# Turning the last 64 queries and keys in a shared bank, scoring in two steps, and a new order within a block of attention

## The chip, the cores and the metric

The kernel runs on one core of one Trainium2 chip. The metric is the device time of one execution in microseconds (us). Every comparison is between runs of the kernel before and after the change on the same chip. The core has five engines that matter here, each with its own instruction stream that it works off in order: TensorE (PE, with its weight loads shown apart as PEld), VectorE (DVE), ScalarE (ACT), GpSimd (POOL) and SyncE (SP), which here only issues DMAs. They wait for each other through semaphores.

## The reference, cut to what matters

```python
# batch 8, heads 8, sequence 576, head dimension 64, all float32
scores = scale * np.matmul(q, k.transpose(0, 1, 3, 2))          # scale 1/8
thresh = np.max(scores, axis=-1, keepdims=True) - tau
scores = np.where(scores >= thresh, scores, -1000000000.0)
scores = scores - np.max(scores, axis=-1, keepdims=True)
attn = np.exp(scores)
attn = attn / (np.sum(attn, axis=-1, keepdims=True) + 1e-09)
attn_out = np.matmul(attn, v)
x = attn_out.transpose(0, 2, 1, 3).reshape(4608, 512)
h = np.maximum(x @ w_in, 0.0)                                     # 512 -> 2048
out = h * h @ w_out                                               # 2048 -> 512
```

## The kernel before, in words

There are three stages, one after the other: attention, the hidden layer (x @ w_in, relu, square) and the output layer. The change touches only attention.

**Pairs, slots and blocks.** Two heads are worked at a time: 32 pairs. The 576 queries of a pair are cut into four tiles of 128 and a last one of 64 (`BLK`, `NB = 5`), so attention is 160 slots, numbered `n = 5 * pair + t`. Five slots of one pair are called a block here, and `s` stands for `n mod 5`. `slot(n)` (L531) is a software pipeline written out by hand: in slot n the scores of slot n+3 are computed, the softmax of n+2 is begun, that of n+1 ended, the weights of n-1 are transposed and the product with v of n-2 is made. The order of the calls in `slot` is the order of the instructions on every engine.

**What a slot issues.** The names that the text uses are these:

- *w*, *W* and *R*: `turn_part(n - 1, ...)`. W transposes the first head's four tiles of weights into a PSUM bank and copies them out on ACT (L427, L429, L432), w does the same for the second head, and R transposes the last 64 columns of both heads (L405). For the last tile of a pair (t = 4), w does nothing.
- *values*: `values_and_load(n - 2)` multiplies with v (L457, L462) into part 0 of a bank named `pvR`; R puts its transpose in part 1 of that bank, and one ACT copy (L408, or L411 with L413 or L417) takes both parts out. In the slots with s = 1 it also issues the loads of a later v (L290, L292).
- *q turn*, *k turn*, *rest turn*: the generator `turn` for the next pair transposes its 512 first queries (bank `pqk`, L303, copied and scaled on ACT by L308), its 512 first keys (L303, L306) and then the last 64 of both together (bank `pqkr`, L311, copied by L312 and L313). GpSimd then copies the 64 keys of the two heads to the diagonal blocks of `kdiag` (L316). q and k turn are in slot s = 0, the rest turn late in slot s = 1, and after it `load` asks SP for the queries and keys of the pair after next (L278, L279).
- *main* and *diagonal*: `ahead(n + 3)` calls `scores`, which makes two main products (L341), one per head, against 512 keys, and one product against `kdiag` for the last 64 keys of both heads (L345). Head 0 ends up in columns 0 to 575 and head 1 in columns 960 to 1535 of a tile `sc` of three banks. For t = 4 there is no diagonal product but four small main ones.
- `stage` and `second` step the softmax generators: two maxima on DVE (L357), a threshold on POOL (L362), two exponentials on ACT (L369), two masked sums on DVE (L374), a tiny add on POOL (L378), a reciprocal on DVE (L380) and two scalings on POOL (L389).
- `convert1` to `convert6` turn one of 32 chunks of the FFN weights from float64 to float32 (a new chunk every second slot; in slots 0 to 34 and 76 to 110). `fetch` loads the raw chunk (L181), `convert1` is its first reader, on ACT (L201). `sums_step` is one POOL addition of weight blocks per slot (L130 or L133) in slots 35 to 79 and 111 to 155.

**Buffers.** [...] two `sc` tiles of three banks, and two single banks (`b_pool`) that every transpose and every product with v takes in turn. A new use of such a bank waits until ACT has copied out the use before the last. So the order in which the banks are asked for, together with ACT's order, decides who waits for whom.

Of the kernel before, what the change touches and what calls it, by code (L numbers as in the profile page):

```python
# [10 lines left out]
FP32 = mybir.dt.float32  # L11
# [37 lines left out]
def kernel(  # L49
# [25 lines left out]
    nc = tc.nc  # L75
# [219 lines left out]
    def turn(i):  # L295

        qn, kn, rn = loaded.pop(i)
        qT = sb.tile([P, S], FP32, tag="qT", bufs=2, name="qT")
        kT = sb.tile([P, S], FP32, tag="kT", bufs=2, name="kT")
        for nat, to in ((qn, qT), (kn, kT)):  # L300
            pt = bank([P, FULL, P], "pqk")
            for t in range(FULL):
                nc.tensor.transpose(pt[:, t, :], nat[:, t, :], ident[:, :])  # L303
            flat, to = pt[:, :, :].rearrange("p t m -> p (t m)"), to[:, 0:MAIN]
            if nat is kn:
                nc.scalar.copy(to, flat)  # L306
            else:
                nc.scalar.activation(out=to, in_=flat, func=AF.Identity, scale=qscale[:, :])  # L308
            yield
        pt = bank([P, P], "pqkr")  # L310
        nc.tensor.transpose(pt[:, :], rn[:, :], ident[:, :])  # L311
        nc.scalar.activation(out=qT[:, MAIN:S], in_=pt[:, 0:REST], func=AF.Identity, scale=qscale[:, :])  # L312
        nc.scalar.copy(kT[:, MAIN:S], pt[:, REST:P])  # L313
        for j in range(2):
            rows = ds(j * D, D)
            nc.gpsimd.tensor_copy(out=kdiag[i % 2][rows, ds(j * REST, REST)], in_=kT[rows, MAIN:S])  # L316
        turned[i] = (qT, kT)

    def scores(i, t):

        qT, kT = turned[i]
        m = BLK[t]
        sc = sc_pool.tile([P, 3 * BANK], FP32, tag="sc", name="sc")
        b_main = 2 * BANK


        one_rest = t < FULL  # L330
        for part in range(1 if one_rest else 2):
            for j in range(2):
                rows = ds(j * D, D)
                k0, n = ((0, MAIN), (MAIN, REST))[part]
                if t == FULL:
                    to = sc[rows, ds(k0, n)]
                elif j == 0:
                    to = sc[:, ds(k0, n)]
                else:
                    to = sc[:, ds((b_main, b_main - REST)[part], n)]  # L340
                nc.tensor.matmul(to, qT[rows, ds(t * P, m)], kT[rows, ds(k0, n)], start=True, stop=True)  # L341
        if one_rest:
            to = sc[:, MAIN:S]
            to = bass.AP(tensor=to.tensor, offset=to.offset, ap=[to.ap[0], [b_main - S, 2], [1, REST]])
            nc.tensor.matmul(to, qT[:, ts(t, P)], kdiag[i % 2][:, :], start=True, stop=True)  # L345
        return sc

    def softmax(i, t, sc):

        nj = 2 if t < FULL else 1  # L350
        at = (0, 2 * BANK - REST)[0:nj]
        sm = sb.tile([P, 2], FP32, tag="sm", bufs=3, name="sm")
        nmx = sb.tile([P, 2], FP32, tag="nmx", bufs=3, name="nmx")
        thr = sb.tile([P, 2], FP32, tag="thr", bufs=3, name="thr")
        w = sb.tile([P, 2 * S], FP32, tag="w", bufs=4, name="w")
        for j in range(nj):
            nc.vector.tensor_reduce(  # L357
                out=nmx[:, j : j + 1], in_=sc[:, ds(at[j], S)], axis=AXIS.X, op=ALU.max, negate=True
            )
            if j == nj - 1:  # L360

                nc.gpsimd.tensor_scalar(  # L362
                    out=thr[:, 0:nj], in0=nmx[:, 0:nj], scalar1=-1.0, scalar2=tau_p[:, :], op0=ALU.mult, op1=ALU.subtract
                )
            yield
        for j in range(nj):
            if j:
                yield
            nc.scalar.activation(  # L369
                out=w[:, ts(j, S)], in_=sc[:, ds(at[j], S)], func=AF.Exp, bias=nmx[:, j : j + 1], scale=1.0  # L370
            )
        for j in range(nj):
            yield
            nc.vector.scalar_tensor_tensor(  # L374
                out=w[:, ts(j, S)], in0=sc[:, ds(at[j], S)], scalar=thr[:, j : j + 1], in1=w[:, ts(j, S)],
                op0=ALU.is_ge, op1=ALU.mult, accum_out=sm[:, j : j + 1],
            )
        nc.gpsimd.tensor_scalar(out=sm[:, 0:nj], in0=sm[:, 0:nj], scalar1=1e-9, scalar2=None, op0=ALU.add)  # L378
        yield
        nc.vector.reciprocal(out=sm[:, 0:nj], in_=sm[:, 0:nj])  # L380
        if t == FULL:

            normalize(w[:, S : S + REST], w[:, MAIN:S], sm[:, 0:1])
        for j in range(nj):
            normalize(w[:, ts(j, S)], w[:, ts(j, S)], sm[:, j : j + 1])
        weights[i, t] = w
# [4 lines left out]
    def transposes(n):  # L391
# [9 lines left out]
        def rest():  # L401


            pt, n_ = pending.pop() if pending else (bank([P, 2, P], "pvR"), 0)
            nc.tensor.transpose(pt[:, 1, :], w[:, ds(MAIN, P)], ident[:, :])  # L405
            xr = sb.tile([P, 2, P], FP32, tag="xr", bufs=3, name="xr")
            if t < FULL and n_ == P:
                nc.scalar.copy(xr[:, :, :], pt[:, :, :])  # L408
            else:
                if n_:  # L410
                    nc.scalar.copy(xr[:, 0, 0:n_], pt[:, 0, 0:n_])  # L411
# [4 lines left out]
                        rows = ds(j * REST, REST)  # L416
                        nc.scalar.copy(xr[rows, 1, at], pt[rows, 1, ds(j * REST, REST)])  # L417
            if n_:
                give_x(n - 1, xr)
            rests[i, t] = xr[:, 1, :]  # L420

        def main(j):
            if j and t == FULL:
# [9 lines left out]

        rows_of[n] = {"R": rest, "W": lambda: main(0), "w": lambda: main(1)}

    rows_of, pending, rests = {}, [], {}

    def turn_part(n, part):

# [6 lines left out]
    def values(i, t):  # L446
# [4 lines left out]
        pt = bank([P, 2, P], "pvR")  # L451
        pv = pt[:, 0, 0:n]

        for c in range(FULL):
# [5 lines left out]
        for j in range(2):  # L460
# [4 lines left out]
        pending.append((pt, n))  # L465

    def give_x(n, xr):
        i, t = slots[n]
# [4 lines left out]
    turning = {}  # L473

    def turn_step(i):
        if i in turning:
            if next(turning[i], 0) == 0 and i + 1 < len(pairs):
                load(i + 1)

    def turn_begin(n):  # L480

        i = n // NB + 1
        if n >= 0 and n % NB == 0 and i < len(pairs):
            turning[i] = turn(i)
            next(turning[i])

    def turn_on(n, at):
        if n >= 0 and n % NB == at:
            turn_step(n // NB + 1)

    def values_and_load(n):

# [17 lines left out]
        if n in jobs and slots[n][1] < FULL:  # L510
            next(jobs[n], None)

    def ahead(n):
        if n < len(slots):
            i, t = slots[n]
            jobs[n] = softmax(i, t, scores(i, t))


    PACE = (2, 1)
# [8 lines left out]
        while summing and next(summing[0], 0) == 0:  # L528
            summing.popleft()

    def slot(n):  # L531

        begun = lambda d: starts.get(n - d)
# [4 lines left out]
        while later:  # L538
            to, from_ = later.popleft()
            nc.sync.dma_start(out=to, in_=from_)  # L540
        turn_begin(n)
        convert4(begun(3))
        turn_part(n - 1, "w")
        values_and_load(n - 2)
        convert1(begun(1))
        turn_part(n - 1, "R")
        stage(n + 2)
        stage(n + 1)
        convert3(begun(2))
        turn_on(n, 0)  # L550
        second(n + 1)
        turn_part(n - 1, "W")
        second(n + 2)
        stage(n + 2)
        sums_step()
        convert5(begun(3))
        convert6(begun(4))
        second(n + 2)
        stage(n + 1)
        turn_on(n, 1)  # L560
        ahead(n + 3)
        convert2(begun(1))
        fetch(begun(-1))


    def inner(product, copy, temp, bank, final, tick):
# [274 lines left out]
                    later.append((to[:, :, b, :], o[row][:, :, i, :]))  # L841


    def flush():
        while later:
            to, from_ = later.popleft()
            nc.sync.dma_start(out=to, in_=from_)

    def spread(work, at):

        n = len(work)
# [3 lines left out]
    with tc.manual_schedule():  # L855
        with ExitStack() as stack:
# [8 lines left out]
            turning[0] = turn(0)  # L865
            for _ in range(3):
                turn_step(0)
            load_v(1)
            for n in range(-3, len(slots)):
                slot(n)  # L870
# [3 lines left out]
                if n > 25:  # L874
                    next(xsums, None)
            n = len(slots)
            values_and_load(n - 2)
            for part in "RWw":
                turn_part(n - 1, part)
            values_and_load(n - 1)  # L880
            pt, m = pending.pop()
            xr = sb.tile([P, 2, P], FP32, tag="xr", bufs=3)
            nc.scalar.copy(xr[:, 0, 0:m], pt[:, 0, 0:m])
            give_x(n - 1, xr)
            for _ in range(60):
                sums_step()
            flush()
        banks = ctx.enter_context(tc.tile_pool(name="banks", bufs=1, space=PSUM))

        def reload(at):  # L890
# [32 lines left out]
        for n in range(NSTEP):  # L923
# [17 lines left out]
            def also(m, at):  # L941
# [8 lines left out]
                if at > 4:  # L950
                    squares_due(0)
                if at == 2:
                    flush()
# [5 lines left out]

            work = [None]  # L960
            output_layer(n, also)
        flush()


def as_float(bits):
# [33 lines left out]
```

## Time and profile before

| | |
|---|---|
| median of 3 runs | 1501.11 us (1499.86 to 1501.19) |
| the profiled execution's own time | 1499.22 us |
| its span, first to last instruction | 1497.4 us |
| granted TensorE clock, mean | 0.998 |
| busy in the span: PE, PEld | 1431.0, 1209.3 us |
| busy in the span: POOL, DVE, ACT | 1051.1, 1004.2, 895.8 us |
| attention, to the first product of the hidden layer | 0 to 694.2 us |
| hidden layer, to the first product of the output layer | 694.2 to 1092.8 us |
| output layer | 1092.8 to 1497.4 us |

The start of L405 marks the slots, because R is issued once in each. From one L405 to the next, a block in the middle of attention looks like this:

| from R of slot s to R of the next | 1 to 2 | 2 to 3 | 3 to 4 | 4 to 0 | 0 to 1 | block |
|---|---|---|---|---|---|---|
| us (block from 300.90) | 4.92 | 3.86 | 3.86 | 3.87 | 4.24 | 20.75 |

A profile line of the timeline has the start in us, the duration, the engine, the line of the kernel, the operation with what it writes and reads, how many instructions were merged in the row, and in square brackets how long the engine had been idle before it and what ended that wait. The ends of PE rows are modelled, so distances between PE rows are taken from start to start.

### The profile page before, as it was taken

What the parts mean: (1) busy time and instruction counts of PE and PEld (TensorE: products, weight loads), DVE (VectorE), ACT (ScalarE), POOL (GpSimd) and SP (SyncE); (2) the same over time, 40 slices, a digit from 0 to 9 for tenths busy, and PEclk for the clock granted to TensorE, in tenths of its full rate; (3) what the DMA queues carried; (4) which work ended last, traced back from release to release, by engine and by line L of the source; (5) the groups of instructions that cost most, each with busy time, mean ns of one, the idle gap of its engine ahead of it and who ended that gap; (6) DMA issues with size and microseconds to landing.
All of it is one profiled execution on the core that took longest, in us unless ns stands there. A gap on an engine that the chain in (4) does not pass through costs nothing.

```text
span 1497.4 us, 35275 instructions
## 1 busy us (share of the span) xinstructions
PE 1431.0 (96%) x12880; PEld 1209.3 (81%) x12880; DVE 1004.2 (67%) x2149; ACT 895.8 (60%) x1792; POOL 1051.1 (70%) x1319
## 2 busy tenths in 40 slices
PE   6999899999999999999999999999999999999998
PEld 4656566666655666667999999999999999999998
DVE  5777666667777666665778777788756666555663
ACT  5887777777877777775666566676553333223330
POOL 3777987777776777773675555666587787777775
PEclk9999999999999999999999999999999999999999
DMA  4435223557343222211323334332994432344411
GB/s 109 117 109 149 63 59 91 163 163 227 97 119 103 63 58 51 58 47 49 132 90 117 114 135 141 114 115 105 352 364 142 142 98 82 108 138 142 142 29 29
DMA packets 212955, 176.89 MB, mean 118 GB/s; under 512 B 99888, under 2 KB 161328, under 8 KB 212784
## 3 DMA queue, kind: packets, MB, share of 16 engines
q1 hardware_dynamic: 212784, 174.65, 37.3%
q8 instruction: 102, 1.67, 0.5%
q14 instruction: 69, 0.57, 0.1%
HBM read 105.12 MB, written 69.47 MB: 117 GB/s over the span
## 4 chain that ended last, share of the span: by engine, by line
PE 76%; DVE 8%; ACT 6%; POOL 4%; issue 2%; DMA 2%; SPq 1%; POOLq 0%; ACTq 0%; DVEq 0%
PE po L810 26%; PE ph L687 23%; PE sc L341 8%; PE pvR L457 7%; PE pwT L427 5%; DVE arena L374 4%; PE sc L345 3%; DVE arena L357 3%; ACT arena L369 2%; PE pvR L405 2%; PE pvR L462 1%; POOL arena L389 1%; DVE arena L133 1%; DMA arena<-in_moe_w_in_dram 1%; PE pqk L303 1%
## 5 line engine op out<-in xcount | busy, mean ns | idle before, releaser
L133 POOL TENSOR_TENSOR arena<-arena 128x512 f32<-128x512 f32 (+1 forms) x315 | 377.9, 1222 | 257.0 <-DVE arena L133 220.6
L687 PE MATMUL ph<-arena,w 128*128 128x128 f32 x3528 | 396.6, 275 | 2.4 <-DVE arena L133 1.6
L810 PE MATMUL po<-w,arena 128*128 128x128 f32 x3528 | 396.3, 275 | 2.1 <-ACT arena L601 1.8
L687 PEld LDWEIGHTS ph<-arena,w 128*128 128x128 f32 x3528 | 394.7, 192 | 4.3 <-DVE arena L133 3.9
L810 PEld LDWEIGHTS po<-w,arena 128*128 128x128 f32 x3528 | 394.7, 192 | 3.6 <-ACT arena L601 2.0
L133 DVE TENSOR_TENSOR arena<-ph,arena 128x512 f32<-128x512 f32 x378 | 255.8, 688 | 93.9 <-PE ph L687 63.3
L357 DVE TENSOR_REDUCE arena<-sc 128x1 f32<-128x576 f32 x288 | 217.3, 755 | 145.8 <-PE sc L345 133.6
L374 DVE SCALAR_TENSOR_TENSOR arena<-sc,arena 128x576 f32<-128x576 f32 x288 | 224.3, 812 | 15.1 <-ACT arena L369 13.9
L389 POOL TENSOR_SCALAR arena<-arena 128x576 f32<-128x576 f32 (+1 forms) x320 | 222.8, 705 | 8.4 <-PE sc L341 1.9
L133 DVE TENSOR_TENSOR arena<-po,arena 128x128 f32<-128x128 f32 x378 | 108.1, 290 | 170.2 <-PE po L810 167.0
L369 ACT ACTIVATE arena<-sc,arena 128x576 f32<-128x576 f32 x288 | 200.5, 745 | 24.6 <-DVE arena L357 12.5
L633 ACT COPY c<-arena 128x512 f32<-128x512 f32 (+1 forms) x303 | 172.7, 579 | 61.4 <-DVE arena L130 55.5
L341 PE MATMUL sc<-arena 64*128 64x512 f32 (+2 forms) x768 | 185.1, 573 | 10.9 <-DVE arena L374 8.7
L427 PE MATMUL pwT<-ident,arena 128*128 128x128 f32 x1152 | 177.3, 276 | 15.8 <-ACT arena L417 7.2
L457 PE MATMUL pvR<-arena 128*64 128x128 f32 (+1 forms) x2560 | 163.2, 268 | 21.8 <-ACT arena L313 20.4
L130 POOL TENSOR_TENSOR arena<-arena 128x512 f32<-128x512 f32 (+1 forms) x138 | 174.6, 1265 | 10.0
L130 DVE TENSOR_TENSOR arena<-arena,c 128x512 f32<-128x512 f32 (+1 forms) x267 | 174.7, 662 | 7.4 <-ACT c L633 6.7
L429 ACT COPY arena<-pwT 128x512 f32<-128x512 f32 x256 | 151.2, 591 | 37.2 <-PE pwT L427 25.5
L457 PEld LDWEIGHTS pvR<-arena 128*64 128x64 f32 x2560 | 127.8, 136 | 51.0 <-ACT arena L313 27.8
L427 PEld LDWEIGHTS pwT<-ident,arena 128*128 128x128 f32 x1152 | 131.3, 141 | 28.7 <-ACT arena L417 14.3
L666 ACT ACTIVATE arena<-arena 128x512 f32<-128x512 f32 x144 | 89.9, 624 | 77.6 <-POOL arena L133 77.6
L601 ACT COPY arena<-po 128x128 f32<-128x128 f32 x63 | 16.7, 265 | 180.1 <-PE po L810 178.1
(49 smaller groups left out, 1147.8 us busy)
## 6 DMA issues: line engine op xcount, KB each, us to landing
g<-arena SPq DMA_DIRECT2D x144, 256.0 KB, 2.0
arena<-g SPq DMA_DIRECT2D x144, 256.0 KB, 4.5
w<-w SPq DMA_DIRECT2D x98, 256.0 KB, 4.5
out_dram<-arena SPq DMA_DIRECT2D x72, 128.0 KB, 2.2
arena<-in_q_dram SPq DMA_DIRECT2D x64, 128.0 KB, 2.6
arena<-in_k_dram SPq DMA_DIRECT2D x64, 128.0 KB, 2.9
arena<-in_v_dram SPq DMA_DIRECT2D x32, 256.0 KB, 2.8
arena<-in_moe_w_out_dram SPq DMA_DIRECT2D x16, 512.0 KB, 4.2
```

Source lines behind the costliest of these rows:

```text
L130: e.tensor_tensor(out=out, in0=x, in1=y, op=ALU.subtract)
L133: e.tensor_tensor(out=out, in0=x, in1=y, op=ALU.add)
L341: nc.tensor.matmul(to, qT[rows, ds(t * P, m)], kT[rows, ds(k0, n)], start=True, stop=True)
L357: nc.vector.tensor_reduce(out=nmx[:, j : j + 1], in_=sc[:, ds(at[j], S)], axis=AXIS.X, op=ALU.max, negate=True)
L369: nc.scalar.activation(out=w[:, ts(j, S)], in_=sc[:, ds(at[j], S)], func=AF.Exp, bias=nmx[:, j : j + 1], scale=1.0)
L374: nc.vector.scalar_tensor_tensor(out=w[:, ts(j, S)], in0=sc[:, ds(at[j], S)], scalar=thr[:, j : j + 1], in1=w[:, ts(j, S)], op0=ALU.is_ge, ...
L389: nc.gpsimd.tensor_scalar(out=out, in0=w, scalar1=r, scalar2=1.0, op0=ALU.mult, op1=ALU.mult)
L427: nc.tensor.transpose(pt[:, c, :], w[:, ds(j * (S + REST) + c * P, P)], ident[:, :])
L457: nc.tensor.matmul(pv[rows, :], va[:, j, c, :], wT[:, j, c, 0:n], start=(c == 0), stop=False, skip_group_check=True)
L633: nc.scalar.copy(c, y)
L687: nc.tensor.matmul(to[:, j, :], W_IN[m, k][:, ts(j, P)], of[k][:, m - 1, :], start=(not more and j == 0), stop=True, skip_group_check=True,)
L810: nc.tensor.matmul(to, g[:, j, :], w[:, j, :], start=(not more and j == 0), stop=(j == 3), skip_group_check=True)
```

## The change

The last 64 queries and keys are no longer transposed into a bank of their own. In slot s = 1 they go to a third part of the `pvR` bank, right after R's transpose, and their copies (ACT, then POOL) follow R's copy. The loads of the pair after next are asked for from there. The scores are made in two calls, the diagonal product first and the main products later. The key turn moves to the end of slot s = 0, between the two. Calls within `slot` are put in another order, the tile `w` has three buffers for four, and the finished values wait in a queue with their slot number.

```diff
         kT = sb.tile([P, S], FP32, tag="kT", bufs=2, name="kT")
+        turning[i] = (qT, kT, rn)
...
-        pt = bank([P, P], "pqkr")
-        nc.tensor.transpose(pt[:, :], rn[:, :], ident[:, :])
...
+    def turn_last(i, pt):
+        qT, kT, rn = turning.pop(i)
+        nc.tensor.transpose(pt, rn[:, :], ident[:, :])
+        def then():
+            nc.scalar.activation(out=qT[:, MAIN:S], in_=pt[:, 0:REST], func=AF.Identity, scale=qscale[:, :])
+            nc.scalar.copy(kT[:, MAIN:S], pt[:, REST:P])
+            for j in range(2):
+                rows = ds(j * D, D)
+                nc.gpsimd.tensor_copy(out=kdiag[i % 2][rows, ds(j * REST, REST)], in_=kT[rows, MAIN:S])
+            turned[i] = (qT, kT)
+            if i + 1 < len(pairs):
+                load(i + 1)
+        return then
+
+    def scores_rest(i, t):
+        sc = sc_pool.tile([P, 3 * BANK], FP32, tag="sc", name="sc")
+        if t < FULL:
+            qT, _ = turned[i]
+            to = sc[:, MAIN:S]
+            to = bass.AP(tensor=to.tensor, offset=to.offset, ap=[to.ap[0], [2 * BANK - S, 2], [1, REST]])
+            nc.tensor.matmul(to, qT[:, ts(t, P)], kdiag[i % 2][:, :], start=True, stop=True)
+        return sc
+
+    def scores(i, t, sc):
...
+        for k0, n in ((0, MAIN),) if t < FULL else ((0, MAIN), (MAIN, REST)):
             for j in range(2):
...
+                to = sc[rows, ds(k0, n)] if t == FULL else sc[:, ds(j * 2 * BANK, n)]
                 nc.tensor.matmul(to, qT[rows, ds(t * P, m)], kT[rows, ds(k0, n)], start=True, stop=True)
...
-        w = sb.tile([P, 2 * S], FP32, tag="w", bufs=4, name="w")
+        w = sb.tile([P, 2 * S], FP32, tag="w", bufs=3, name="w")
...
-            pt, n_ = pending.pop() if pending else (bank([P, 2, P], "pvR"), 0)
+            pt, n_, of = pending.popleft() if pending else (bank([P, 3, P], "pvR"), 0, None)
             nc.tensor.transpose(pt[:, 1, :], w[:, ds(MAIN, P)], ident[:, :])
+            then = turn_last(i + 1, pt[:, 2, :]) if t == 0 and i + 1 in turning else None
...
             rests[i, t] = xr[:, 1, :]
+            if then:
+                then()
...
+    TURN_AT = (0, 0)
...
     def slot(n):
...
+        sums_start(n)
+        ask()
         turn_part(n - 1, "w")
+        convert4(begun(n - 3))
+        convert3(begun(n - 2))
+        stage(n + 2)
+        turn_step(n, 0)
         values_and_load(n - 2)
-        convert1(begun(1))
+        convert1(begun(n - 1))
+        stage(n + 1)
+        second(n + 1)
         turn_part(n - 1, "R")
+        second(n + 2)
+        sums_step()
+        turn_part(n - 1, "W")
+        convert6(begun(n - 4))
         stage(n + 2)
+        second(n + 2)
+        fetch(begun(n + 1))
+        convert5(begun(n - 3))
+        ahead(n + 3, 0)
         stage(n + 1)
...
+        turn_step(n, 1)
+        ahead(n + 3, 1)
+        convert2(begun(n - 1))
```

The removed lines of `slot` are those of L538 to L563 above. `ask` is the former `flush`: it issues the DMAs that wait in `later`. `turn_step(n, 0)` is the q turn and `turn_step(n, 1)` the k turn, both in slots with s = 0. The start and the end of attention make the same calls through the new functions.

More of the change, by code (lines that the diff above doesn't have):

```diff
@@ L309, in turn @@
             yield
-        pt = bank([P, P], "pqkr")
[L311 to L319, printed above, removed]
+    def turn_last(i, pt):
[11 more added lines that the diff above has]
+        return then
@@ L324, in scores @@
+    def scores_rest(i, t):
[7 more added lines that the diff above has]
+    def scores(i, t, sc):
         qT, kT = turned[i]
         m = BLK[t]
-        sc = sc_pool.tile([P, 3 * BANK], FP32, tag="sc", name="sc")
@@ L327, in scores @@
-        b_main = 2 * BANK
-        one_rest = t < FULL
-        for part in range(1 if one_rest else 2):
+        for k0, n in ((0, MAIN),) if t < FULL else ((0, MAIN), (MAIN, REST)):
             for j in range(2):
                 rows = ds(j * D, D)
[L334 to L346, printed above, removed]
+                to = sc[rows, ds(k0, n)] if t == FULL else sc[:, ds(j * 2 * BANK, n)]
+                nc.tensor.matmul(to, qT[rows, ds(t * P, m)], kT[rows, ds(k0, n)], start=True, stop=True)
     def softmax(i, t, sc):
@@ L401, in rest @@
         def rest():
-            pt, n_ = pending.pop() if pending else (bank([P, 2, P], "pvR"), 0)
+            pt, n_, of = pending.popleft() if pending else (bank([P, 3, P], "pvR"), 0, None)
             nc.tensor.transpose(pt[:, 1, :], w[:, ds(MAIN, P)], ident[:, :])
+            then = turn_last(i + 1, pt[:, 2, :]) if t == 0 and i + 1 in turning else None
             xr = sb.tile([P, 2, P], FP32, tag="xr", bufs=3, name="xr")
             if t < FULL and n_ == P:
-                nc.scalar.copy(xr[:, :, :], pt[:, :, :])
+                nc.scalar.copy(xr[:, :, :], pt[:, 0:2, :])
             else:
@@ L418, in rest @@
             if n_:
-                give_x(n - 1, xr)
+                give_x(of, xr)
             rests[i, t] = xr[:, 1, :]
+            if then:
+                then()
         def main(j):
@@ L434, in transposes @@
         rows_of[n] = {"R": rest, "W": lambda: main(0), "w": lambda: main(1)}
-    rows_of, pending, rests = {}, [], {}
+    rows_of, pending, rests = {}, deque(), {}
     def turn_part(n, part):
@@ L450, in values @@
         n = BLK[t]
-        pt = bank([P, 2, P], "pvR")
+        pt = bank([P, 3, P], "pvR")
         pv = pt[:, 0, 0:n]
@@ L464, in values @@
             )
-        pending.append((pt, n))
+        pending.append((pt, n, NB * i + t))
     def give_x(n, xr):
@@ L472, with turn_step @@
     slots = [(i, t) for i in range(len(pairs)) for t in range(NB)]
[L473 to L489, printed above, removed]
+    turning, turns = {}, {}
+    TURN_AT = (0, 0)
+    def turn_step(n, at):
+        i, left = divmod(n - TURN_AT[at], NB)
+        i += 1
+        if left == 0 and 0 < i < len(pairs):
+            if at == 0:
+                turns[i] = turn(i)
+            next(turns[i])
     def values_and_load(n):
@@ L511, in second, with ahead @@
             next(jobs[n], None)
[L513 to L516, printed above, removed]
+    def ahead(n, part):
+        if not 0 <= n < len(slots):
+            return
+        i, t = slots[n]
+        if part == 0:
+            jobs[n] = scores_rest(i, t)
+        else:
+            scores(i, t, jobs[n])
+            jobs[n] = softmax(i, t, jobs[n])
     PACE = (2, 1)
@@ L529, in sums_step, with ask, sums_start @@
             summing.popleft()
-    def slot(n):
-        begun = lambda d: starts.get(n - d)
+    def ask():
+        while later:
+            to, from_ = later.popleft()
+            nc.sync.dma_start(out=to, in_=from_)
+    def sums_start(n):
         if n == OUT_SUMS:
@@ L537, in slot, with begun @@
             summing.append(sums(W_IN, SUMS_A, AT_A, lambda m: None))
[L538 to L542, printed above, removed]
+    def begun(n):
+        return starts.get(n)
+    def slot(n):
+        sums_start(n)
+        ask()
         turn_part(n - 1, "w")
+        convert4(begun(n - 3))
+        convert3(begun(n - 2))
+        stage(n + 2)
+        turn_step(n, 0)
         values_and_load(n - 2)
-        convert1(begun(1))
+        convert1(begun(n - 1))
+        stage(n + 1)
+        second(n + 1)
         turn_part(n - 1, "R")
+        second(n + 2)
+        sums_step()
+        turn_part(n - 1, "W")
+        convert6(begun(n - 4))
         stage(n + 2)
+        second(n + 2)
+        fetch(begun(n + 1))
+        convert5(begun(n - 3))
+        ahead(n + 3, 0)
         stage(n + 1)
[L549 to L563, printed above, removed]
+        turn_step(n, 1)
+        ahead(n + 3, 1)
+        convert2(begun(n - 1))
     def inner(product, copy, temp, bank, final, tick):
@@ L841, in output_layer @@
                     later.append((to[:, :, b, :], o[row][:, :, i, :]))
[L844 to L847, printed above, removed]
     def spread(work, at):
@@ L864 @@
             load_v(0)
-            turning[0] = turn(0)
-            for _ in range(3):
-                turn_step(0)
+            for _ in turn(0):
+                pass
+            turn_last(0, bank([P, P], "pqkr")[:, :])()
             load_v(1)
@@ L876, with drain @@
             n = len(slots)
+            def drain():
+                while pending:
+                    pt, m, of = pending.popleft()
+                    xr = sb.tile([P, 2, P], FP32, tag="xr", bufs=3)
+                    nc.scalar.copy(xr[:, 0, 0:m], pt[:, 0, 0:m])
+                    give_x(of, xr)
+            drain()
             values_and_load(n - 2)
@@ L880 @@
             values_and_load(n - 1)
[L881 to L884, printed above, removed]
+            drain()
             for _ in range(60):
                 sums_step()
-            flush()
+            ask()
         banks = ctx.enter_context(tc.tile_pool(name="banks", bufs=1, space=PSUM))
@@ L952, in also @@
                 if at == 2:
-                    flush()
+                    ask()
                 if at == 6:
@@ L961 @@
             output_layer(n, also)
-        flush()
+        ask()
 def as_float(bits):
```

## The prediction

> **What bounds the kernel now.** I read the totals by stage first, then the starts of L405 as a clock for the slots, then the timeline of one block. Totals by stage (length; busy time and instructions of PE, PEld, DVE, ACT, POOL; clock; DMA):
>
> ```profile
> 0.00:694.00 694.00, 638.27 (x5824) 419.93 (x5824) 474.94 (x1090) 506.73 (x1057) 513.22 (x878) 1.00 0.36 100
> 694.00:1088.00 394.00, 392.75 (x3498) 391.23 (x3499) 301.64 (x474) 251.20 (x450) 231.68 (x185) 1.00 0.40 140
> ```
>
> The hidden layer leaves PE no gap. In attention PE is busy 638 of 694 us, so 56 us at most are to be had there, unless PE itself gets less to do, and the change removes no product. No other engine passes 74%. So the question is where PE waits.
>
> An ordinary slot takes 3.86 us from R to R, and its pieces, start to start, fill it: W 0.53, main 1.06, diagonal 0.33, w 0.53, values 1.25, R 0.17, sum 3.87. No wait is left there. The slots beside the turns are longer: 4.92 us from s = 1 to 2, with pieces R 0.17, rest turn 0.17, W 0.53, the four main products of t = 4 1.12, w 0.53, values 1.25, sum 3.77; and 4.24 us from s = 0 to 1, with pieces R, k turn 0.53, W, main, diagonal, w, values of 64 columns 0.74, sum 3.89. So PE waits 1.15 and 0.35 us per block. The timeline shows for what. Slots 1 and 2:
>
> ```profile
> 301.69 0.14 PEld L311 LDWEIGHTS pqkr<-ident,arena 128*128 128x128 f32 x1 [0.27 <-ACT arena L413]
> ...
> 302.83 1.37 ACT L369 ACTIVATE arena<-sc,arena 128x576 f32<-128x576 f32 x2 [0.49 <-DVE arena L380]
> ...
> 303.24 0.66 PE L427 MATMUL pwT<-ident,arena 128*128 128x128 f32 x4
> ...
> 304.09 0.32 ACT L312 ACTIVATE arena<-pqkr,qscale 128x64 f32<-128x64 f32 x1
> 304.29 0.22 ACT L313 COPY arena<-pqkr 128x64 f32<-128x64 f32 x1
> ...
> 304.56 1.10 PE L457 MATMUL pvR<-arena 128*64 128x128 f32 x16 [0.67 <-ACT arena L313]
> ```
>
> The rest turn's bank is copied out by L312 and L313, which stand in ACT's queue behind both exponentials. The values of slot 2 want that bank. They start 1.32 us after w, where 0.53 is needed: 0.79 lost. The rest is 0.11 before L311 and 0.25 before the main products. The page says how general the large wait is:
>
> ```profile
> L457 PE MATMUL pvR<-arena 128*64 128x128 f32 (+1 forms) x2560 | 163.2, 268 | 21.8 <-ACT arena L313 20.4
> ```
>
> Slot 0:
>
> ```profile
> 317.57 0.60 PE L303 MATMUL pqk<-ident,arena 128*128 128x128 f32 x4
> ...
> 317.93 0.42 ACT L417 COPY arena<-pvR 64x64 f32<-64x64 f32 x2
> ...
> 318.41 0.66 PE L427 MATMUL pwT<-ident,arena 128*128 128x128 f32 x4 [0.24 <-ACT arena L417]
> 319.00 1.13 PE L341 MATMUL sc<-arena 64*128 64x512 f32 x4
> ...
> 319.69 1.39 ACT L369 ACTIVATE arena<-sc,arena 128x576 f32<-128x576 f32 x2
> 320.06 0.49 PE L345 MATMUL sc<-arena 128*128 128x128 f32 x2
> 320.27 0.47 PEld L427 LDWEIGHTS pwT<-ident,arena 128*128 128x128 f32 x4
> 320.38 0.60 PE L427 MATMUL pwT<-ident,arena 128*128 128x128 f32 x4
> ```
>
> W waits 0.31 here for the bank that L417 empties.
>
> **The rest turn into the bank of R.** It has the same instructions; one use of a bank per block goes, and with it the wait of slot 2. In slot 1, with R at 0: rest turn at 0.17, W at 0.34, main at about 0.9. L312 and L313 follow R's copies at about 0.65 and are done by 1.1; W's copy (needs W, 0.34 + 0.70) runs 1.05 to 1.64, the exponentials to 3.0. PE ends main and w at 2.55, and the values' bank is W's, free at 1.64. What is late next is DVE: main needs the second sum (L374) of the same slot. It ended at 1.15 before (322.80 against R at 321.65). L357 now starts behind main, with no diagonal behind that, so I take 0.9 to 1.0 and a wait of 0.1. R to R: 0.17 + 0.17 + 0.53 + 0.1 + 1.12 + 0.53 + 1.25 = 3.87 for 4.92. This happens for 31 pairs: 31 x 1.05 = **32.5 us gained**.
>
> On POOL, L316 (0.53) now stands before the threshold L362, the sum step (1.27) and the scalings (1.47), and it waits for L313. From 1.15 that is 0.53 + 0.31 + 1.27 + 1.47, to 4.75 after R. The scaled weights are wanted by w of slot 3, at 3.87 + 2.1 = 5.97. So 1.2 us of cover hide it; the cost is nil until they are gone.
>
> **The k turn to the end of slot 0.** With R at 0: W at 0.17 without its wait, diagonal at 0.7, k turn at 1.0 (its bank is free when L417 is done, R + 1.0), main at 1.6, w at 2.65, values ready at 3.2. On ACT, W's copies start at 0.93, the exponentials at 1.45 and L306 behind them at 2.71 (1.26 for two); it takes 0.59. The values of slot 1 want k's bank: 3.35, so a **new wait of 0.15** takes over. R to R 3.35 + 0.74 = 4.09 for 4.24, 30 times: 4 us gained. Behind the waiting L306 ACT holds only w's copy, wanted 1.2 us later.
>
> **Diagonal first.** L345 runs where main began, and both need the sums of slot n+1 done, since the whole `sc` tile is released at once (main of t = 4, which writes none of the columns last read, waited for L374 all the same). L357 starts 0.04 us after the diagonal now, and then behind main; as PE hands over in the same time, DVE gains 0.1 us, which nobody waits for in ordinary slots. PE's price is its weight loads. Before: W to main and main to diagonal show exposed loads (load and product start together), diagonal to w does not: the load at 320.27 starts under L345, 0.11 before its product. After: W to diagonal and main to w. By the rows, loads stay hidden between two 128x128 products and are exposed where the shape changes; the count of exposed ones is the same, so **0**. The Trainium skill speaks against the move ("TensorE: Matmul & The Clock Gate", Part 3, The mechanism): weight loads overlap running products only when the row group differs. By it, W to diagonal would stay exposed and main to w too, some 0.11 us more in each of 128 full slots: 14 us lost. The row 320.27 shows the overlap within the same 128 rows, so I take the row; ends -6 and +14.
>
> **The rest of the order.** DVE's order is the same. ACT's is, but for L306, L312 and L313. Three `w` buffers cost nothing: L369 of n+2 overwrites what w, R and W of n-1 have read, and W's copy ahead of it on ACT waits for those anyway. SP's order (`ask`, v loads, q and k loads, `fetch`) stays.
>
> **What is given back.** In six blocks (`fetch` in slots 1, 11, 21, 81, 91, 101) SP issues the raw chunk behind nine loads, after slot 1's values: at 368.88, 5.7 us after R at 363.14. ACT's L201 two slots on waits for it, and all copies behind L201 with it:
>
> ```profile
> 373.47 0.67 ACT L201 ACTIVATE arena<-arena 128x512 f32<-128x512 f32 x1 [2.05 <-DMA arena<-in_moe_w_in_dram]
> ```
>
> Nothing of the change brings that transfer nearer to R of slot 1, so these blocks gain nothing from slot 1 to 4: 6 x 1.05 = 6.3 us. Blocks 5 to 7 (130 to 197 us) carry conversion and x sums; in 152.6 to 175.5 POOL is busy 21.4 of 22.9 us, so half a us each is not to be had: 1.5. The other five converting blocks have ACT at 17.5 of what would be 19.6 us: 0.2 each, 1.
>
> **Sum**: 32.5 + 4 - 6.3 - 1.5 - 1 = 27.7 us. From the profiled execution's 1499.22: 1471.5; the median stands 1.9 above it, so 1473.4.
>
> **Rivals.**
>
> 1. *Exposed loads.* The rule holds: 27.7 - 14 leaves 13.7, **1487**. For it, main to diagonal is exposed today; against it, 320.27. Chance 0.15.
> 2. *All waits go.* The raw chunk and POOL cost nothing because a loosened block lets SP run ahead, or the new order hides loads: 36.5 gained, **1464**. Against it, SP starts after the values. Chance 0.2.
> 3. *The new wait becomes the bound, slower.* Place: L306 behind the exponentials, the values of slot 1 behind L306. It costs 0.15 at my numbers. If W's copies or the maxima come late, so does L306, and each us goes to PE in 30 blocks. From 0.92 us on (27.7 / 30) it outweighs all gains; with 1.2 us, **1510**. For it: ACT must run five operations in a row there; against it, these ran just so at 319.16 to 321.08 and with 0.2 us of idle time before. Chance 0.1.
> 4. *Nothing lands*, because another wait of the same length sits behind L313, 1501. DVE's second sum ends 0.1 late by my sum, not 1.15. Chance 0.05.
>
> My forecast has the remaining 0.5. The range takes in 1 and 2: 1463 to 1489. Less than 0.2%, 3 us, can't be told from no change; chances: faster 0.85, same 0.04, slower 0.11.
>
> **What will show it.** Right: L457's idle time for L313 (20.4 us) gone, R to R 3.9 from slot 1 to 2, a wait of 0.1 to 0.3 us for L306's successor at the values of slot 1, ordinary slots still 3.86, L201's waits for DMA longer by about 1 us. Wrong: ordinary slots of 3.97 (rival 1), or values in slot 1 a us late (rival 3).

## The result, and the profile after

| | before | after |
|---|---|---|
| median, 4 runs each | 1500.52 us (1499.86 to 1501.19) | 1488.11 us (1484.56 to 1489.47) |
| profiled execution, its span | 1499.22, 1497.4 us | 1488.86, 1487.0 us |

The ratio is 0.9912, with a 95% interval of 0.9897 to 0.9927: 12.4 us faster, where 27.7 were forecast.

The wait that the sum was built on went as it said. The costliest groups of the kernel after, busy time and mean, then the idle time before the instructions:

```profile
L467 PE MATMUL pvR<-arena 128*64 128x128 f32 (+1 forms) x2560 | 164.2, 269 | 5.0 <-ACT arena L439 0.7
```

These are the products with v: 21.8 us of idle time before them became 5.0, and L313's 20.4 are gone. A block in the middle of attention, from one R to the next (R is L412 now):

| from slot to slot | 1 to 2 | 2 to 3 | 3 to 4 | 4 to 0 | 0 to 1 | block |
|---|---|---|---|---|---|---|
| before | 4.92 | 3.86 | 3.86 | 3.87 | 4.24 | 20.75 |
| forecast | 3.87 | 3.86 | 3.86 | 3.87 | 4.09 | 19.55 |
| after (from 508.73) | 3.85 | 4.23 | 3.82 | 3.93 | 4.16 | 19.99 |

Slot 1 to 2 is as forecast to 0.02 us. A third of its gain is lost again in the next interval. In the kernel before, the second masked sum was done well ahead of the products that need it (slot 2 of the block from 300.90, the sum and then the main products):

```profile
305.05 0.81 DVE L374 SCALAR_TENSOR_TENSOR arena<-sc,arena 128x576 f32<-128x576 f32 x1
...
306.51 1.13 PE L341 MATMUL sc<-arena 64*128 64x512 f32 x4
```

The sum ended at 305.86, so 0.65 us were to spare, less than the 1.05 us by which slot 2 was to come forward. The timeline of the kernel after, slots 1 and 2 of the block from 488.74 (start, length, engine, line):

```profile
489.48 0.33 ACT L318 ACTIVATE arena<-pvR,qscale 128x64 f32<-128x64 f32 x1
...
490.33 1.37 ACT L376 ACTIVATE arena<-sc,arena 128x576 f32<-128x576 f32 x2
...
490.86 0.76 DVE L364 TENSOR_REDUCE arena<-sc 128x1 f32<-128x576 f32 x1 [0.55 <-PE sc L353]
...
491.81 0.82 DVE L381 SCALAR_TENSOR_TENSOR arena<-sc,arena 128x576 f32<-128x576 f32 x1 [0.19 <-ACT arena L376]
...
492.55 0.81 DVE L381 SCALAR_TENSOR_TENSOR arena<-sc,arena 128x576 f32<-128x576 f32 x1
...
492.75 0.60 PE L437 MATMUL pwT<-ident,arena 128*128 128x128 f32 x4
...
493.52 0.46 PE L338 MATMUL sc<-arena 128*128 128x128 f32 x2 [0.17 <-DVE arena L381]
493.91 1.13 PE L353 MATMUL sc<-arena 64*128 64x512 f32 x4
```

Slot 3 of the same block has no such wait, and shows where L338 would start without it:

```profile
496.97 0.60 PE L437 MATMUL pwT<-ident,arena 128*128 128x128 f32 x4
497.30 0.30 PEld L338 LDWEIGHTS sc<-arena 128*128 128x128 f32 x2
...
497.41 0.39 PE L338 MATMUL sc<-arena 128*128 128x128 f32 x2
...
497.73 1.13 PE L353 MATMUL sc<-arena 64*128 64x512 f32 x4
```

Read the timeline of slots 1 and 2 from its end upward. In slot 3 the diagonal product L338 starts 0.44 us after W (497.41 for 496.97) and the main products 0.32 after it. In slot 2 it is 0.77 (493.52 for 492.75) and 0.39: together 0.40 us more, which is the difference between 4.22 and 3.82. L338 waits for the second masked sum, which ends at 492.55 + 0.81 = 493.36. The first masked sum had its maximum at 491.62 (490.86 + 0.76) and started at 491.81, 0.11 after the exponentials of slot 1 ended (490.33 + 1.37 = 491.70). The first of those two was done near 491.07, so the sums wait for both. PE came forward by 1.07 us against R of slot 1, the end of the exponentials by only 0.34 (R + 3.30 before, from 302.83 + 1.37, and R + 2.96 now).

Slot 4, same kernel:

```profile
500.37 0.82 DVE L381 SCALAR_TENSOR_TENSOR arena<-sc,arena 128x576 f32<-128x576 f32 x1
...
501.25 0.30 PEld L338 LDWEIGHTS sc<-arena 128*128 128x128 f32 x2
501.25 0.49 PE L338 MATMUL sc<-arena 128*128 128x128 f32 x2
...
501.67 1.13 PE L353 MATMUL sc<-arena 64*128 64x512 f32 x4
```

Here the sum ends at 501.19 and the load of L338 follows at 501.25, at the same time as its product instead of 0.11 ahead of it under W. Slot 4 has become as long as DVE's ring: maximum to the end of the second sum 2.3, diagonal to main 0.42, main to the next maximum 1.18.

Two more places where time went. The start: before, the first scores were main products; now the first thing is the diagonal one, and it needs GpSimd's copies. The timeline of the kernel before, and then that of the kernel after:

```profile
8.41 2.08 PE L341 MATMUL sc<-arena 64*128 64x512 f32 x4 [0.46 <-ACT arena L306]
```

```profile
9.20 0.52 POOL L322 COPY arena<-arena 64x64 f32<-64x64 f32 x2 [7.38 <-ACT arena L319]
9.77 0.80 PE L338 MATMUL sc<-arena 128*128 128x128 f32 x2 [1.45 <-POOL arena L322]
```

The first R comes at 26.07 for 23.01, of which the order explains a part (see start_main_first). And the blocks with a late raw chunk, here block 18 of the kernel after; then the same place by stretches of 2 us (length; busy time and instructions of PE, PEld, DVE, ACT, POOL; granted clock; DMA share and GB/s):

```profile
413.63 0.66 ACT L201 ACTIVATE arena<-arena 128x512 f32<-128x512 f32 x1 [4.04 <-DMA arena<-in_moe_w_in_dram]
...
414.69 1.05 PE L437 MATMUL pwT<-ident,arena 128*128 128x128 f32 x4 [2.55 <-ACT arena L416]
```

```profile
412.00:414.00 2.00, 0.14 (x2) 0.00 (x0) 0.76 (x1) 0.37 (x1) 0.92 (x2) 1.00 0.97 367
414.00:416.00 2.00, 1.31 (x8) 1.01 (x10) 0.00 (x0) 2.00 (x5) 0.65 (x1) 0.68 0.20 68
416.00:418.00 2.00, 2.00 (x20) 1.67 (x17) 1.59 (x5) 1.34 (x3) 0.00 (x0) 0.50 0.00 0
```

L201 waits 4.04 us for the chunk, 2.62 before. PE stands still for 2.55 us, and after that it runs for some 3.4 us at half its clock (0.50): L437's four transposes take 1.05 us in place of 0.6.

The account of the profiled executions, from R to R over all blocks:

| | forecast | measured |
|---|---|---|
| slot 1 to 2 | -32.5 | -32.9 |
| slot 2 to 3 | 0 | +12.1 |
| slot 3 to 4, late chunks in it | +6.3 | +5.8 |
| slot 4 to 0 | 0 | +2.0 |
| slot 0 to 1 | -4.0 | -1.2 |
| other converting blocks, blocks 5 to 7 | +2.5 | in the rows above |
| start | 0 | +3.1 |
| end of attention and later stages | 0 | +0.8 |
| sum | -27.7 | -10.3 |

### The profile page after: what moved, and what is told of

Read it like the earlier page. It is cut to its first block, busy times and chain, and to the rows that moved or that the text cites. A ratio compares the mean times of both kernels' runs of the same rounds, so it can differ in the third digit from the quotient of the medians.

```text
span 1487.0 us, 35254 instructions
## 1 busy us (share of the span) xinstructions
PE 1437.3 (97%) x12880; PEld 1214.7 (82%) x12880; DVE 1006.9 (68%) x2149; ACT 888.9 (60%) x1792; POOL 1052.9 (71%) x1319
## 4 chain that ended last, share of the span: by engine, by line
PE 61%; DVE 15%; ACT 8%; POOL 6%; DMA 5%; issue 3%; SPq 1%; POOLq 0%; DVEq 0%; ACTq 0%
PE po L829 27%; PE ph L706 21%; DVE arena L381 9%; ACT arena L376 5%; PE sc L353 5%; DVE arena L364 4%; PE pvR L467 3%; PE pwT L437 3%; PE sc L338 2%; POOL arena L396 1%; DVE arena L133 1%; DMA w<-w 1%; POOL w L130 1%; ACT arena L307 1%; POOL arena L133 1%
## 5 line engine op out<-in xcount | busy, mean ns | idle before, releaser
L381 DVE SCALAR_TENSOR_TENSOR arena<-sc,arena 128x576 f32<-128x576 f32 x288 | 224.5, 813 | 21.8 <-ACT arena L376 21.2
L437 PEld LDWEIGHTS pwT<-ident,arena 128*128 128x128 f32 x1152 | 128.6, 141 | 90.5 <-issue 36.2
L437 PE MATMUL pwT<-ident,arena 128*128 128x128 f32 x1152 | 181.5, 280 | 12.9 <-ACT arena L416 9.5
```

The lines of the kernel that those rows point to most:

```text
L381: nc.vector.scalar_tensor_tensor(out=w[:, ts(j, S)], in0=sc[:, ds(at[j], S)], scalar=thr[:, j : j + 1], in1=w[:, ts(j, S)], op0=ALU.is_ge, ...
L437: nc.tensor.transpose(pt[:, c, :], w[:, ds(j * (S + REST) + c * P, P)], ident[:, :])
```

## The experiments

Theory A after the result: once the wait of slot 1 is gone, the scores of slot 2 come too early for DVE's masked sums, whatever the order of the products; the start and the late chunks are costs of their own. Theory B: the diagonal product first is what costs. C, D and E stand in the expectations. The median before was 1500.6 to 1501.1 us in these comparisons.

| kernel | 1 to 2 | 2 to 3 | 3 to 4 | 4 to 0 | 0 to 1 | block | first R | median us | ratio to before |
|---|---|---|---|---|---|---|---|---|---|
| rest_in_R | 4.18 | 4.01 | 3.86 | 3.87 | 4.24 | 20.17 | 23.34 | 1490.93 | 0.992 to 0.995 |
| main_first | 4.18 | 4.01 | 3.86 | 3.87 | 4.24 | 20.16 | 23.42 | 1490.12 | 0.9901 to 0.9941 |
| diag_first_only | 4.90 | 3.86 | 3.82 | 3.94 | 4.20 | 20.71 | 24.71 | 1502.28 | 1.0001 to 1.0023 |
| k_turn_late_only | 4.92 | 3.86 | 3.86 | 3.87 | 4.24 | 20.75 | 25.04 | 1501.29 | 0.9998 to 1.0017 |
| chunk_early | 3.85 | 4.23 | 3.82 | 3.94 | 4.16 | 20.00 | 26.77 | 1473.71 | 0.9803 to 0.9836 |
| exp_early | 3.85 | 3.94 | 3.82 | 3.94 | 4.16 | 19.72 | 27.13 | 1483.28 | 0.9865 to 0.9894 |
| start_main_first | 3.85 | 4.23 | 3.82 | 3.94 | 4.16 | 20.00 | 24.84 | 1486.25 | 0.9887 to 0.9917 |
| three_together | 3.85 | 3.94 | 3.82 | 3.94 | 4.16 | 19.72 | 24.83 | 1466.60 | 0.976 to 0.979 |
| sums_first_s2 | 3.85 | 4.21 | 3.82 | 3.93 | 4.16 | 19.97 | 24.41 | 1487.48 | 0.9891 to 0.9936 |
| three_sums_first_s2 | 3.85 | 3.82 | 3.82 | 3.94 | 4.16 | 19.59 | 23.91 | 1462.85 | 0.9733 to 0.9762 |
| three_s4_main_first | 3.85 | 3.94 | 3.82 | 3.86 | 4.16 | 19.63 | 23.40 | 1463.35 | 0.9736 to 0.9765 |
| five_together | 3.85 | 3.82 | 3.82 | 3.86 | 4.17 | 19.52 | 24.27 | 1460.06 | 0.9714 to 0.9746 |

**The rest turn alone.** `slot` in the order of before, scores in one step, main first, k turn early; the three `w` buffers stay:

```diff
-        pt = bank([P, P], "pqkr")
-        nc.tensor.transpose(pt[:, :], rn[:, :], ident[:, :])
...
+            then = turn_last(i + 1, pt[:, 2, :]) if t == 0 and i + 1 in turning else None
```

> The kernel before with the rest turn alone moved into R's bank (order of a slot, scores in one step and k turn as before). Theory A (once the wait of slot 1 is gone, the scores of slot 2 come too early for DVE's second masked sum, which stands behind the exponentials of slot 1; the order of the products has no part in it): R to R 3.9 us from slot 1 to 2, 4.1 from 2 to 3, 4.24 from 0 to 1, a block of 19.9, start as before, the five blocks with a late chunk no shorter: about 1482. Theory B (the diagonal product first is what costs in slots 2 and 4): 3.9, then 3.86 from 2 to 3, a block of 19.7: about 1476.

L313's wait is gone, and slots 1 to 3 take 8.19 us, where A had 8.0 and B 7.76. So the new wait does not need the diagonal first. It stands in both slots here; in slot 1 of this kernel:

```profile
514.60 1.19 PE L352 MATMUL sc<-arena 64*64 64x512 f32 x8 [0.35 <-DVE arena L380]
```

The main products wait 0.35 us for the second masked sum. The bank alone gives 10.1 us (1490.93 for 1501.05), most of the 12.4 of the whole change. The time missed A's number by 9 us, the profiled execution (1493.70) by 12. In that execution the five blocks with a late chunk got about 5 us longer (three of their slots took over 7 us), six converting blocks took 4.51 from slot 2 to 3, about 3 us in all, and an ordinary block took 20.17 for A's 19.9.

**Main first in the kernel after.**

```diff
-        ahead(n + 3, 0)
         stage(n + 1)
         turn_step(n, 1)
-        ahead(n + 3, 1)
+        ahead(n + 3)
```

> The kernel after with the scores in one step again, main products first, at the place of the main products. Theory A: from slot 2 to 3 4.1 to 4.2 us still, from 4 to 0 back to 3.87, the first R 1.4 to 3 us earlier, blocks with a late chunk as in the kernel after: about 1484. Theory B: 3.86 from 2 to 3 and 3.87 from 4 to 0, a block of 19.6: about 1474.

Slot 2 to 3 falls by 0.22 but slot 1 to 2 rises by 0.33; slot 4 to 0 goes back to 3.87 and the first R to 23.42. B falls: with the order undone the pair of intervals is longer, 8.19 for 8.08. A's mechanism holds, but not its time (1490.12 for 1484): it had taken slot 1 to 2 to stay at 3.85. What the diagonal first brings there is a head start for DVE: the first maximum of slot 1 starts 1.39 us before R in the kernel after (507.34 to 508.73) and 1.06 us before it here (524.66 to 525.72), because PE hands over both scores at main and only then waits for L307.

**The raw chunk early.**

```diff
         turn_step(n, 0)
+        fetch(begun(n + 1))
         values_and_load(n - 2)
...
-        fetch(begun(n + 1))
```

> The kernel after with the load of the raw chunk put ahead of the loads of v, q and k in SP's queue (before the values of its slot). Theory A (the chunk lands 10.5 us after R of slot 1 because SP issues it behind nine loads, so faster slots only lengthen L201's wait, and the long gap costs TensorE its clock once): L201 waits for no DMA outside the first slots, blocks 2, 4, 16, 18 and 20 take 20.0 to 20.6 us in place of 22.4 to 24.0: about 1476. Rival C (the transfers themselves are the limit, so the wait moves to the v, q or k loads): no change or slower, about 1488.

The instructions of L201 in this kernel, with what they waited for:

```profile
L201 ACT ACTIVATE arena<-arena x32: 673/704/743, 27.5 to 457.9; 128x512 f32<-128x512 f32 x32
its engine sat idle before it (us, times) until:
  DMA arena<-in_moe_w_in_dram: 1.0, 1
```

One wait of 1.0 us is left of six with 18.3 in all. The five blocks take 20.0 us each, and 14.4 us of median time go. C falls: the transfers were not the limit, their place in SP's queue was. On the kernel after, this one line is worth more than the whole change was on the kernel before; on the kernel before it was not tried.

**The first exponential of slot 1 early.** In slot s = 1 it stands before R's copies on ACT; that order needs a fourth `w` buffer, and `softmax` yields accordingly (not shown).

```diff
+        if n % NB == 1:
+            stage(n + 2)
         turn_part(n - 1, "R")
...
         stage(n + 2)
-        second(n + 2)
+        if n % NB != 1:
+            second(n + 2)
```

> The kernel after with the first exponential of slot 1 put ahead of R's copies on ACT, into 0.65 us in which ACT is idle (and four w buffers, which this order needs). Theory A: the exponentials of slot 1 end 0.6 us sooner, the masked sums of slot 2 start 0.2 us sooner (then bound by the maximum before them), R to R from 2 to 3 falls from 4.22 to 4.0: about 1482. Theory B: 4.22 stays, about 1488.

The timeline of that kernel, R of slot 1 at 545.22:

```profile
544.95 0.75 ACT L365 ACTIVATE arena<-sc,arena 128x576 f32<-128x576 f32 x1
...
546.77 0.76 ACT L365 ACTIVATE arena<-sc,arena 128x576 f32<-128x576 f32 x1
...
547.36 0.76 DVE L370 TENSOR_REDUCE arena<-sc 128x1 f32<-128x576 f32 x1 [0.55 <-PE sc L353]
...
548.03 0.81 DVE L389 SCALAR_TENSOR_TENSOR arena<-sc,arena 128x576 f32<-128x576 f32 x1
```

The sums start 2.81 us after R for 3.07 before, straight behind the maximum, and slot 2 to 3 takes 3.94. Theory A's 4.0 and 1482 stand (3.94 and 1483.28); B's 4.22 does not. The fourth buffer by itself was not tried, but the rows show the sums coming forward with the exponential.

**Two parts of the change alone, on the kernel before.**

```diff
+        if one_rest:
+            ...
+            nc.tensor.matmul(to, qT[:, ts(t, P)], kdiag[i % 2][:, :], start=True, stop=True)
         for part in range(1 if one_rest else 2):
```

> The kernel before with the diagonal product put ahead of the main ones, nothing else. Theory A (the move gives DVE 0.1 us in each slot, which nobody waits for while L313 holds slot 2 back, and it makes the first scores of all wait for GpSimd's copies to kdiag): the first R 2 to 3 us later, slot 1 to 2 still 4.9, slot 4 to 0 at 3.94 for 3.87 (DVE's ring of maximum, two masked sums, diagonal, main products), 1503 to 1506. Theory B (the move is what pays from slot 1 to 2): 4.6 or less there, about 1492.

```diff
-        turn_on(n, 0)
         second(n + 1)
...
+        turn_on(n, 0)
         turn_on(n, 1)
         ahead(n + 3)
```

> The kernel before with the k turn moved to the end of slot 0, ahead of the scores, nothing else. Theory A: W's wait of 0.31 goes and the values of slot 1 wait 0.2 us for the copy behind the exponentials; 4.15 to 4.25 from slot 0 to 1 for 4.24, 1497 to 1502. Rival D (the move is worth its full 0.31 us, and the new wait comes from the rest of the order): 3.93, about 1491.

Neither pays alone. The diagonal first gives back in slot 4 and at the start what it saves in slots 3 and 0. The late k turn exchanges one wait for another of the same length (4.24 both ways). Its first R is 2.0 us late in the profiled execution; how much of that is the order is not shown (see the next experiment).

**Main first for the first pair.**

```diff
-            jobs[n] = scores_rest(i, t)
+            jobs[n] = sc_pool.tile([P, 3 * BANK], FP32, tag="sc", name="sc")
+            if i:
+                scores_rest(i, t, jobs[n])
         else:
             scores(i, t, jobs[n])
+            if not i:
+                scores_rest(i, t, jobs[n])
```

> The kernel after with the main products first for the first pair alone. Theory A (the start is 3 us late because the first diagonal product waits for GpSimd's copies to kdiag, and all other work behind it): the first R about 2.7 us earlier, at 23.4, all later blocks as in the kernel after, 1485.5. Rival: the late start is of another origin (the loads, or the k turn at the end of slot 0): R at 26, 1488.

The first R comes 1.2 us earlier than after (24.84), not 2.7. This does not settle the shares, because the first R also moves with the granted clock. The traces record stretches at 0.50 before it: one of 3.4 us before the change, 6.8 us in the kernel after, 10.2 us here. sums_first_s2, below, issues the same instructions as the kernel after up to the first R, and has only 3.4 us. The main products ahead of the first R, in the kernel after and then in sums_first_s2:

```profile
23.56 2.08 PE L353 MATMUL sc<-arena 64*128 64x512 f32 x4
```

```profile
22.77 1.13 PE L353 MATMUL sc<-arena 64*128 64x512 f32 x4
```

Its first R is at 24.41. Five kernels have 3.4 us at 0.50 in their traces there, and can be compared: before 23.01; main_first, main products first for all pairs, 23.42; three_s4_main_first and three_sums_first_s2, which have this edit, 23.40 and 23.91; sums_first_s2, diagonal first, 24.41. So the order costs about 1.4 us at the start, 0.5 to 1.0 of it by the diagonal first, and the other 1.7 of the 3.1 go with the clock, but for the 0.2 by which the first scores already started later (9.77 for 9.53). The medians, 1486.25 for 1488.11, fit a gain of 1 us or so, but their ranges overlap.

**The three edits together.**

> The kernel after with the raw chunk's load early, the first exponential of slot 1 early and the main products first for the first pair. If the three costs are apart from each other, their gains add up: 14.4 + 4.8 + 2.7 below the kernel after, 1466. If they share a wait, it stays above 1470.

1466.60 where 1466 was expected: they add up.

**Which wait is last in slot 2.** The two masked sums ahead of the maximum there, on the kernel after and on the version with three edits:

```diff
-        stage(n + 2)
+        if n % NB != 2:
+            stage(n + 2)
...
         second(n + 1)
+        if n % NB == 2:
+            stage(n + 2)
```

> The kernel after with the two masked sums ahead of the maximum on DVE in slot s = 2. Theory A' (the masked sums of slot 2 wait for BOTH exponentials of slot 1, which end later than that maximum): nothing moves, 4.2 from slot 2 to 3, 1488. Rival E (DVE's own work, the maximum ahead of the sums, is what makes them late): 3.9 or less from slot 2 to 3, 1478.

> The version with three edits, and the two masked sums ahead of the maximum in slot s = 2. Theory A' (with the exponential early, that maximum is the last thing ahead of the sums): slot 2 to 3 falls from 3.94 to 3.82, 3.5 us less, 1463. Rival E: no further gain, 1466.5.

The first of these two, slots 1 and 2:

```profile
509.70 1.37 ACT L376 ACTIVATE arena<-sc,arena 128x576 f32<-128x576 f32 x2
...
511.16 0.82 DVE L381 SCALAR_TENSOR_TENSOR arena<-sc,arena 128x576 f32<-128x576 f32 x1 [1.48 <-POOL arena L369]
```

DVE now has nothing to do for 1.48 us, and still starts only at 511.16, 0.09 after the second exponential (509.70 + 1.37). The bracket names a POOL instruction that had ended 0.9 us earlier; as both come through one wait, the one that ended last counts. Alone the edit is worth nothing (4.21 from 2 to 3). With the exponential early it is worth 0.12 per block and slot 2 to 3 is at 3.82, PE's own length. So one wait lay behind the other, as A' had it.

**DVE's ring in slot 4.** Main first there:

```diff
-            if i:
+            if i and t != 2:
                 scores_rest(i, t, jobs[n])
...
-            if not i:
+            if t < FULL and (not i or t == 2):
                 scores_rest(i, t, jobs[n])
```

> The version with three edits, and in slot s = 4 the main products ahead of the diagonal one. Theory A (with the diagonal first, slot 4 is as long as DVE's ring: maximum, two masked sums, diagonal, main products, 3.94 us; with main first it is 3.87): slot 4 to 0 at 3.87, the others as they are, 2 us less, 1464.5. Rival: 3.94 stays, or the 0.07 us come back in slot 0.

3.86, and nothing came back in slot 0.

> All five edits on the kernel after. If the gains add up: 1461 to 1462, a block of 19.53.

1460.06 us, 2.7% below the kernel before and 28 us below the kernel after. A block of 19.52 is what the forecast had for the change by itself (19.55).

## Why the prediction was wrong

- **The step that failed** is the end of the rest turn's part, "31 x 1.05 = 32.5 us gained": with slot 1 to 2 at 3.87, the sum counted the whole 1.05 us and left the next interval as it had been, and expected "ordinary slots still 3.86". It asked what is late next only in the slot where the stall went, and found DVE 0.1 us late. It did not shift slot 2 forward by the 1.05 us and ask again, though the second masked sum there had only 0.65 us to spare. In slot 2 the masked sums wait for both exponentials of slot 1, at R + 2.96 by the trace; the working had that end at 3.0, and never carried it to the sums behind it. It cost 0.36 us in each of 31 blocks, with one longer case 12.1 us of the 17.4 by which the table misses the forecast. exp_early and three_sums_first_s2 take it back in two parts, 0.28 and 0.12.
- **The ring.** Before, DVE's ring and PE's slot had the same length, 3.87 (the maximum at 315.83 follows that at 311.96), so a change of 0.1 us in it was not free. The forecast priced the diagonal first at "DVE gains 0.1 us"; in slot 4 it lost 0.07, since DVE now waits for both products of a slot behind its own last sum. three_s4_main_first shows it.
- **The start** was left at nothing. The forecast named GpSimd's copies for slot 1 only. Measured 3.1 us in the profiled execution; about 1.4 of it come with the order, and the rest mostly with a second stretch at half the clock, which sums_first_s2, with the same order there, did not have.
- **Slot 0 to 1** was mis-sized: the copy behind the exponentials is done at R + 3.38, not 3.30, and the gain was 0.08 per block for 0.15. (30 times 0.15 is also 4.5, where the sum has 4.) Alone, the move is worth 0.
- **The late chunks** came out near in size (5.8 for 6.3), in part by luck. Six blocks were named and five were late: in block 0 L201 did not wait. Where 1.05 us was taken for each, from slot 3 to 4 three of the five lost 0.55 to 0.80 and blocks 16 and 18 lost 1.64 and 2.64. In these two the chunk did not keep its distance from R, as the forecast had it: it landed at R + 11.3 for 10.3, and R + 11.6 for 11.2.
- **Right**: slot 1 to 2 (3.85 for 3.87), the cover on POOL, the three buffers, and L201's waits in the five blocks (longer by 1.0 us on average, 0.6 to 1.7). The loads of the weights, too: ordinary slots took 3.82, where the rule of the Trainium skill that the prediction weighed ("TensorE: Matmul & The Clock Gate", Part 3, The mechanism) would have made it 3.97. The trace goes against that rule: the load of L338 at 497.30 starts under W's transposes, 0.11 us before its own product, within the same 128 rows.
- **The rivals**: 1 did not come. 2 did not come either: SP did not run ahead, and L201's waits went only when the load was moved by hand, in chunk_early. 3 was the right kind of thing, a new wait behind the exponentials, in the wrong slot and for DVE. 4 had a wait for DVE behind that for L313, of the same length; it came in the slot after, and 0.4 us long.

## What to carry to other kernels

When a stall goes, shift everything behind it forward by its length and check each later wait again, for one whole round of the pipeline: another engine that used to finish under the stall may now be last. Where two engines' rounds are equally long, a reordering that lengthens either one shows in the time. A load that stands behind others in one DMA queue can become the limit when the kernel gets faster; here moving it by one line gave 14.4 us, where the change itself had given 12.4.

## What the runs showed of the hardware that was not expected

Gaps of about 2 us on PE are sometimes followed by a halved clock. After 2.55 us idle in block 18 the granted clock was 0.50 for 3.4 us; a gap of 2.21 us in block 16 of the same execution had no such effect. Between 30 and 1400 us the fourteen traces have eleven stretches at 0.50, each 3.4 us long, and each begins within 1.4 us of the end of a PE gap of 1.80 to 2.55 us. Eighteen other gaps of 1.80 to 2.31 us were followed by none, nor were any of the 21 gaps between 1.3 and 1.8 us (ends of PE rows are modelled, so the lengths are rough).

What a stretch costs is not settled. In block 18, 4.4 us passed from L201's start to the next R, against 2.9 in block 16; but the next slot was 1.0 us shorter (3.87 for 4.84), and over the two slots both blocks lost 1.8 us against the kernel before. It agrees with the scatter that the kernels on the order of after with late chunks spread by 1.4 to 7.3 us over their runs, chunk_early and what is built on it by 0.4 to 2.5. No run changed the gap alone, so this link is read from the traces and not shown by an experiment.
